# A retention + ELU kernel on one Trainium2 core: the first four chunks taken pair by pair, v scaled on GpSimd for two of them, and the fifth first-layer tile in two parts

## The chip, the core and the metric

The kernel runs on one core of a Trainium2 chip. A core has a matrix engine (TensorE, "PE" in the profile, with its weight loads as "PEld"), three engines that work on whole tiles (VectorE "DVE", ScalarE "ACT", GpSimd "POOL") and SyncE ("SP"), which here issues every DMA transfer. Each engine runs its own queue in order and waits for the others through semaphores. The metric is device time in microseconds of one execution, as a median over several.

## The reference

Two blocks follow each other. The first is a retention layer on q, k, v of shape (4 batches, 8 heads, 768 positions, 64 channels):

```python
for t in range(S):
    state = gamma * state + outer(k[t], v[t])      # per batch and head, gamma = 1 - 2**(-5-h)
    y[t] = q[t] @ state / sqrt(D)
```

Its output, read as x of shape (3072 tokens, 512), goes through a two-layer network with an ELU between:

```python
h = x @ w_in            # 512 -> 2048
g = where(h > 0, h, exp(min(h, 0)) - 1)
out = g @ w_out         # 2048 -> 512
```

q, k and v are float32. w_in and w_out are float64 and reach the chip as bit patterns.

## The kernel before

Tokens are worked in six blocks (`tb`) of 512 tokens, each of four chunks of 128 positions. A chunk has its q and k turned (`qk`) and its k and v as they are (`kvn`), each 0.5 MB and loaded by one DMA. Chunks of a block are taken in two pairs (`pp` = 0 and 1; `x` is the chunk in the pair), and a chunk is two halves (`sub`) of 64 positions.

**Retention of a pair.** `scale_v` multiplies v by the powers of 1/gamma (v'). `scores` (L260) forms k q^T for both halves and VectorE masks it (L273) into the place of k in `qk`. `states` (L279) forms k^T v' per half on TensorE (L290) and adds it to the state of the half before (L301, or a ScalarE copy, L299, where no state goes before); the new state is written over the k that has just been used, so state n+1 of a chunk lies in the first or second half of that chunk's k. `outputs` (L303) has three steps, run by `next(y)`: the masked scores times v' (L314) and the first half of the products of q with the states (L338, `other` = 0); then a small VectorE read of both accumulators (L326, `seen`) and the second half of the products (`other` = 1); then the multiplication by powers of gamma into `xb`, the network's input (L345).

**PSUM.** Pool `ps_r` has four buffers, given out in turn: for the first pair two to the scores, two to the states, and then two to the outputs, which are the buffers of the scores again.

**Weights.** There are 16 pieces of 1 MB: eight of w_in, then eight of w_out. `prepare` (ScalarE, L142 and L144) and `decode` (four VectorE operations, L163 to L166) turn a piece from float64 bits into float32; a piece may be taken in two parts of 512 columns. Three pieces may be staged at once, so the load of a further piece (L121) waits on SyncE for the decode that frees a buffer, and all later loads wait behind it.

**The first block.** `plain_first` (L402) forms the 16 tiles of h for block 0. Its first four tiles are done in two halves of 256 tokens, so that half 0 (the first pair) can go before the second pair's outputs are there: tiles 0 and 1 (bank `pa`, weights `w_a`[0]), tile 2 (`pb`) and tile 3 (`pd`, both of `w_b`[0]), L409. The other twelve are done with all 512 tokens at once (L420). Their ELU is two ScalarE operations (L390, L391) and one on VectorE (L394).

Each engine's order is the order in which the program issues. The order at the start is written out by hand (the lines after `second_twice`, ending in the loop over `inner`): prepare piece 0, decode its first part, scale chunks 0 and 1, scores of the first pair, decode the second part, states, prepare piece 1, outputs, scale chunk 2, decode piece 1, scale chunk 3, prepare piece 2, tiles 0 and 1 of half 0, scores and states of the second pair, first part of piece 2's decode, tiles 2 and 3 of half 0, outputs of the second pair, second part of the decode, and then the rest of the tiles with a piece decoded at every second one. v' is made on VectorE for chunks 0 and 2, by eight ScalarE operations each for chunks 1 and 3, and on GpSimd for all later ones (L242).

After block 0 the blocks use a seven-product scheme (`strassen`, `second`, `first_twice`, `second_twice`), with the retention of the next block spread between; the change leaves those lines as they are.

Of the kernel before, what the change touches and what calls it, by code (L numbers as in the profile page):

```python
# [9 lines left out]
FP32 = mybir.dt.float32  # L10
# [3 lines left out]
ALU = mybir.AluOpType  # L14
# [3 lines left out]
def kernel(  # L18
# [32 lines left out]
    nc = tc.nc  # L51
    PSUM = bass.MemoryType.PSUM
    P = nc.NUM_PARTITIONS

    B, H, S, D, DM, DFF = dims
# [3 lines left out]
    TH = TB // 2  # L59
    HP = H // 2  # L60
# [3 lines left out]
    CPB = TB // C  # L64
# [84 lines left out]

    quarters = lambda f: scratch.rearrange("(s k) p (f c) -> k f p s c", k=2, f=4)[f // 4, f % 4]  # L150

    def decode():

        n = len(decoded)
        if n >= NPIECE:
            return
        dst, todo = prepared[n]
        decoded.append(dst.rearrange("p (a b) -> p a b", a=2))
        vec = nc.vector
        for c, hi, flat in todo:  # L160
            cf = c.bitcast(FP32)

            vec.tensor_scalar(cf, cf, 122879.9921875, 2.0**-15, ALU.min, ALU.max)  # L163
            vec.tensor_scalar(c, c, 3, 0x3FFFFFF8, ALU.logical_shift_left, ALU.bitwise_and)
            vec.scalar_tensor_tensor(c, hi, 0xC0000000, c, ALU.bitwise_and, ALU.bitwise_or)
            vec.tensor_tensor(out=flat, in0=c, in1=flat, op=ALU.add)  # L166
# [81 lines left out]
    def state(tb, n):  # L248

        if n % (2 * CPB) == 0:  # L250
            return carry[(tb + n // (2 * CPB)) % 2]

        k = raw[tb * CPB + (n - 1) // 2][1][:, 0].rearrange("p h d -> p (h d)")
        return k[:, (n - 1) % 2 * 256 : ((n - 1) % 2 + 1) * 256].rearrange("p (h e) -> p h e", e=D)

    def fresh(tb, n):

        return (tb * 2 * CPB + n) % (S // D) == 0

    def scores(tb, pp):  # L260

        two = [raw[tb * CPB + 2 * pp + x][0] for x in range(2)]
        sc = [ps_r.tile([P, 2, HP, D], FP32, name="sc", tag="r") for _ in range(2)]
        for x, qk in enumerate(two):
            for p in range(HP):
                for sub in range(2):
                    for a in range(2):
                        nc.tensor.matmul(
                            sc[a][rows(sub), x, p, :], lhsT=qk[rows(a), 1, p, rows(sub)],
                            rhs=qk[rows(a), 0, p, rows(sub)], start=True, stop=True, skip_group_check=True,  # L270
                        )
        for a in range(2):
            nc.vector.tensor_tensor(  # L273
                out=two[a][:, 1].rearrange("p h c -> p (h c)").rearrange("p (n t) -> p n t", t=D),
                in0=sc[a].rearrange("p x h t -> p (x h) t"),
                in1=cmask.unsqueeze(1).to_broadcast([P, 2 * HP, D]), op=ALU.mult,
            )

    def states(tb, pp):  # L279

        kvs = [ps_r.tile([P, 2, HP, D], FP32, name="kv", tag="r") for _ in range(2)]
        order = [(x, sub) for x in range(2) for sub in range(2)]
        last = lambda x, sub: fresh(tb, 4 * pp + 2 * x + sub + 1)
        for x in range(2):
            kv = raw[tb * CPB + 2 * pp + x][1]
            for p in range(HP):
                for sub in range(2):
                    for a in range(2):
                        if not last(x, sub):
                            nc.tensor.matmul(  # L290
                                kvs[sub][rows(a), x, p, :], lhsT=kv[rows(sub), 0, 2 * p + a, :],
                                rhs=kv[rows(sub), 1, 2 * p + a, :], start=True, stop=True, skip_group_check=True,
                            )
        for x, sub in order:
            n = 4 * pp + 2 * x + sub
            if last(x, sub):
                continue
            if fresh(tb, n):
                nc.scalar.copy(state(tb, n + 1), kvs[sub][:, x])  # L299
            else:  # L300
                nc.vector.tensor_tensor(out=state(tb, n + 1), in0=kvs[sub][:, x], in1=state(tb, n), op=ALU.add)  # L301

    def outputs(tb, pp):  # L303

        y = [ps_r.tile([P, 2 * 2, 2, D], FP32, name="y", tag="r") for _ in range(2)]
        for x in range(2):
            kv = raw[tb * CPB + 2 * pp + x][1]
            for j in range(4):
                a, u = divmod(j, 2)
                pt = raw[tb * CPB + 2 * pp + a][0][:, 1].rearrange("p h c -> p (h c)")  # L310
                for sub in range(2):
                    for c in range(2):
                        p = 2 * u + c
                        nc.tensor.matmul(  # L314
                            y[sub][rows(c), j, x, :], lhsT=kv[rows(sub), 1, head(a, u, c), :],
                            rhs=pt[rows(sub), (x * HP + p) * D : (x * HP + p + 1) * D],
                            start=(x == 0 and j == 0), stop=False, skip_group_check=True,
                        )
        for other in range(2):
            if not other:  # L320
                yield
            else:

                for sub in range(2):
                    seen = epool.tile([P, 8], FP32, name="seen", tag="seen")
                    nc.vector.tensor_copy(seen.rearrange("p (j x) -> p j x", x=2), y[sub][:, :, :, 0])  # L326
                yield
            for x in range(2):
                q = raw[tb * CPB + 2 * pp + x][0]
                for u in range(2):  # L330
                    for a in range(2):
                        sub = a ^ other
                        n = 4 * pp + 2 * x + sub
                        if fresh(tb, n):
                            continue
                        for c in range(2):
                            p = 2 * u + c
                            nc.tensor.matmul(  # L338
                                y[sub][rows(c), 2 * a + u, x, :], lhsT=state(tb, n)[rows(a), p, :],
                                rhs=q[rows(a), 0, p, rows(sub)], start=False, stop=True, skip_group_check=True,  # L340
                            )
        i = chunks[tb * CPB + 2 * pp][1]
        for sub in range(2):
            place = lambda t: t.rearrange("p j (x s c) -> p j x s c", x=2, s=2)[:, :, :, sub, :]
            nc.vector.tensor_tensor(  # L345
                out=place(xb[:, :, 2 * pp * C : 2 * (pp + 1) * C]), in0=y[sub],
                in1=place(etab.rearrange("p a u t -> p (a u) t")[:, :, i * C : (i + 2) * C]), op=ALU.mult,
            )
# [53 lines left out]
    def plain_first():  # L402
# [1 line left out]
        tiles = [(n, w, row, fi) for n in range(NQ) for w, row in ((w_a, 0), (w_b, 1)) for fi in range(2)]  # L404
        banks = [bank(x) for x in "aabd"]
        for t in range(2):
            for (n, w, row, fi), hp in zip(tiles, banks):
                for j in range(4):
                    nc.tensor.matmul(  # L409
                        hp[:, t, :], lhsT=w[n][:, fi, j // 2, j % 2, :], rhs=xb[:, j, half[t]],  # L410
                        start=(j == 0), stop=(j == 3), skip_group_check=True,
                    )
                if t == 1:
                    elu(g_plain[row * NF + 2 * n + fi], hp.rearrange("p a b -> p (a b)"))
                if t == 1 or fi == 1:
                    yield
        for n, w, row, fi in tiles[4:]:
            hp = ps_r.tile([P, TB], FP32, name="hp", tag="r")
            for j in range(4):
                nc.tensor.matmul(  # L420
# [525 lines left out]
    next(y)  # L946
    next(y)
    next(y, None)
    next(piece)
    next(piece, None)  # L950
    prepare()
# [230 lines left out]
```

## Time and profile before

| what | value |
|---|---|
| median of 5 executions | 651.57 us (650.21 to 653.41) |
| the profiled execution | 653.41 us, the longest of the five; span 651.6 us |
| mean granted TensorE clock | 0.995 |
| TensorE busy | 633.2 us (97%) |
| VectorE, ScalarE, GpSimd busy | 469.5, 237.7, 37.0 us |
| moved by DMA | 134.16 MB, mean 206 GB/s |

The profiled execution lasted 1.8 us longer than its span; that is time outside the first and the last instruction. In the timeline views a row gives the start in us from the span's start, the time from the first start to the last end of a run of like instructions, engine, line, operation, the tiles, shapes, the count, and in brackets the idle time before it and what ended it. One matrix product of the program shows as two MATMUL and two LDWEIGHTS rows. "issue" is idle time for which the profile shows nothing that was waited for. In the table of windows, PEclk is the share of the TensorE clock that was granted.

### The profile page before, as it was taken

To read this page: it belongs to the slowest core of one execution; us is meant where nothing else is said; L and a number is where in the kernel's file an instruction comes from. 1 tells how busy PE (TensorE), PEld (TensorE's weight loads), DVE (VectorE), ACT (ScalarE), POOL (GpSimd) and SP (SyncE) were. 2 spreads that over 40 slices of the span, in tenths; PEclk is the share of its full clock that TensorE was granted. 3 is DMA by queue.
4 is the path that set the end of the run, shared out by engine and by line. 5 is a ranking of instruction groups with operands and counts; after the bars stand their busy time and mean duration, and the time that the engine had idled before them with its cause. 6 is when DMAs were issued, how large, how long until landed. Compare 5 with 4: busy or idle time off the path is not lost.

```text
span 651.6 us, 15255 instructions
## 1 busy us (share of the span) xinstructions
PE 633.2 (97%) x6336; PEld 538.9 (83%) x6336; DVE 469.5 (72%) x829; ACT 237.7 (36%) x447; POOL 37.0 (6%) x36
## 2 busy tenths in 40 slices
PE   4889999999999999999999999999999999999998
PEld 3664445548888889989989988999988999988997
DVE  5688778757866845489857578958569958557976
ACT  7466733104542001455111455311355311256311
POOL 1000100000540000020000020000020000000000
PEclk9799999999999999999999999999999999999999
DMA  8638979537293784931778830688850588610694
GB/s 341 242 130 287 308 238 278 146 103 258 65 323 137 245 298 156 375 134 34 246 244 280 289 155 4 205 267 283 281 210 3 174 268 266 226 56 1 209 307 164
DMA packets 69012, 134.16 MB, mean 206 GB/s; under 512 B 5712, under 2 KB 23504, under 8 KB 66640
## 3 DMA queue, kind: packets, MB, share of 16 engines
q1 hardware_dynamic: 68944, 133.19, 60.6%
q8 instruction: 50, 0.82, 0.5%
q14 instruction: 18, 0.15, 0.1%
HBM read 109.05 MB, written 24.12 MB: 204 GB/s over the span
## 4 chain that ended last, share of the span: by engine, by line
PE 96%; DMA 1%; DVE 1%; issue 1%; SPq 0%; DVEq 0%
PE pa L780 16%; PE pa L741 10%; PE pd L780 8%; PE hp L420 6%; PE pa L695 4%; PE pa L434 4%; PE pa L579 4%; PE pb L741 4%; PE pa L521 4%; PE pb L780 4%; PE qa L741 3%; PE pd L695 2%; PE pd L579 2%; PE qd L741 2%; PE pd L521 2%; PE pd L741 2%
## 5 line engine op out<-in xcount | busy, mean ns | idle before, releaser
L788 ACT COPY ms<-pa 128x128 f32<-128x128 f32 x83 | 22.1, 266 | 114.8 <-PE pa L780 114.8
L391 ACT ACTIVATE r<-r 128x512 f32<-128x512 f32 x96 | 60.5, 630 | 3.1
L780 PE MATMUL pa<-ts,wq 128*128 128x128 f32 x448 | 59.2, 275 | 0.0
L780 PE MATMUL pd<-ts,wq 128*128 128x128 f32 x440 | 58.2, 275 | 0.0
L780 PEld LDWEIGHTS pa<-ts,wq 128*128 128x128 f32 x448 | 54.8, 192 | 0.2
L780 PEld LDWEIGHTS pd<-ts,wq 128*128 128x128 f32 x440 | 53.5, 192 | 0.2 <-DVE res L792 0.2
L780 PE MATMUL pa<-gC,wq 128*128 128x128 f32 x384 | 51.9, 278 | 1.6 <-issue 1.6
L390 ACT ACTIVATE r<-gC 128x512 f32<-128x512 f32 x64 | 39.9, 624 | 33.8 <-DVE gC L749 33.8
L780 PEld LDWEIGHTS pa<-gC,wq 128*128 128x128 f32 x384 | 47.3, 192 | 2.7 <-issue 1.7
L394 DVE SCALAR_TENSOR_TENSOR gC<-r,gC 128x512 f32<-128x512 f32 x64 | 45.8, 748 | 0.7 <-ACT r L391 0.7
L242 POOL TENSOR_TENSOR kvn<-kvn,vf 128x512 f32<-128x512 f32 x20 | 23.0, 1154 | 361.8 <-DMA kvn<-in_qkv_dram 197.8
L471 ACT COPY m<-pa 128x512 f32<-128x512 f32 x27 | 15.7, 581 | 60.8 <-PE pa L579 35.5
L792 DVE TENSOR_TENSOR res<-pd,ms 128x128 f32<-128x128 f32 x54 | 15.4, 286 | 29.0 <-PE pd L780 28.4
L657 DVE TENSOR_TENSOR ts<-gC,ts 128x512 f32<-128x512 f32 x48 | 33.0, 687 | 0.8
L657 DVE TENSOR_TENSOR ts<-gC 128x512 f32<-128x512 f32 x48 | 32.7, 682 | 0.0
L434 PE MATMUL pa<-gC,w_s 128*128 128x512 f32 x64 | 30.6, 600 | 0.0
L579 PE MATMUL pa<-gC,ws 128*128 128x256 f32 x128 | 28.6, 381 | 0.0
L579 PEld LDWEIGHTS pa<-gC,ws 128*128 128x128 f32 x128 | 24.1, 190 | 3.4
L780 PE MATMUL pb<-gC,wq 128*128 128x128 f32 x192 | 26.4, 277 | 0.1
L780 PEld LDWEIGHTS pb<-gC,wq 128*128 128x128 f32 x192 | 23.7, 192 | 0.8 <-DVE gC L394 0.8
L749 DVE TENSOR_TENSOR gC<-qa,gC 128x512 f32<-128x512 f32 x8 | 5.5, 692 | 25.1 <-PE qa L741 18.3
L813 ACT COPY res<-pa 128x128 f32<-128x128 f32 x27 | 7.2, 266 | 44.7 <-PE pa L780 42.3
(199 smaller groups left out, 1293.2 us busy)
## 6 DMA issues: line engine op xcount, KB each, us to landing
wq<-scratch_dram SPq DMA_DIRECT2D x228, 256.0 KB, 4.3
wraw<-in_w_dram SPq DMA_DIRECT2D x16, 1024.0 KB, 5.8
qk<-in_qkv_dram SPq DMA_DIRECT2D x24, 512.0 KB, 7.2
kvn<-in_qkv_dram SPq DMA_DIRECT2D x24, 512.0 KB, 7.9
scratch_dram<-so SPq DMA_DIRECT2D x22, 512.0 KB, 3.2
ws<-scratch_dram SPq DMA_DIRECT2D x7, 1024.0 KB, 7.9
scratch_dram<-w_s SPq DMA_DIRECT2D x8, 512.0 KB, 7.1
out_dram<-res SPq DMA_DIRECT2D x11, 256.0 KB, 4.3
```

The source lines that it names most:

```text
L242: eng.tensor_tensor(out=kv[:, 1], in0=kv[:, 1], in1=vf[:, i].unsqueeze(2).to_broadcast([C, H, D]), op=ALU.mult)
L390: nc.scalar.activation(e, h, AF.Relu, scale=-1.0)
L391: nc.scalar.activation(e, e, AF.Exp, scale=-1.0)
L394: nc.vector.scalar_tensor_tensor(g, e, -1.0, h, ALU.add, ALU.max)
L420: nc.tensor.matmul(hp, lhsT=w[n][:, fi, j // 2, j % 2, :], rhs=xb[:, j, :], start=(j == 0), stop=(j == 3))
L434: nc.tensor.matmul(ops[d], lhsT=wo[:, row, d * P : (d + 1) * P], rhs=g_plain[row * NF + f], start=(f == 0 and row == 0), stop=(f == NF - 1 ...
L521: nc.tensor.matmul(ps[:, fi, :], lhsT=w[:, fi, j2, :], rhs=x[:, j2, :], start=(begin and fi == 0 and j2 == 0), stop=(j2 == 1), skip_group_ ...
L579: nc.tensor.matmul(ps[:, d, :], lhsT=ws[:, 2 * d + f // 4, f % 4, :], rhs=gq[INPUT2[j]][:, f, :], start=(begin and f == 0 and d == 0), sto ...
L657: sub = lambda o, x, y: nc.vector.tensor_tensor(out=o, in0=x, in1=y, op=ALU.subtract)
L695: nc.tensor.matmul(ps[:, f, :], lhsT=lhs[f], rhs=xs[j][k], start=(begin and f == 0), stop=True, skip_group_check=True,)
L741: nc.tensor.matmul(ps[:, fi, :], lhsT=w[:, fi, j2, :], rhs=x[:, j2, :], start=(j in (1, 7) and fi == 0 and j2 == 0), stop=(j2 == 1), skip_ ...
L780: nc.tensor.matmul(ps, lhsT=w[:, f, :], rhs=ts[j][k][:, f, :], start=(begin and f == 0), stop=(f == 3), skip_group_check=True,)
```

## The change

- **First pair by chunks.** Scores, masks, states and outputs of block 0's first pair are issued chunk by chunk: scores of chunk 0, its mask, its k^T v', then scores of chunk 1, the states after chunk 0, the mask of chunk 1. The mask becomes four operations of 128x256 in place of two of 128x512, and a chunk's masked scores lie in its own `qk`. The outputs become five steps: L314's products of chunk 0, those of chunk 1, then the two halves of the state products, then the multiplication into `xb`.
- **k^T v' of chunk 1** is split by half: that of its first half goes between the two chunks' L314 products, that of its second half behind the outputs' last product, and its addition behind the multiplication into `xb`. The state between the two halves (state 3) goes to `xt[0]`, which is free then, since k is still needed.
- **v'** of chunks 1 and 2 is made on GpSimd (before: eight ScalarE operations, and one on VectorE). Chunk 0 stays on VectorE and chunk 3 on ScalarE.
- **Decode of piece 0** can be stopped after each VectorE operation: the second part's first two operations go behind the mask of chunk 1, the third behind the addition of state 3, the fourth behind the `seen` copies.
- **Tile 4** of `plain_first` (`w_a`[1], first 512 columns of piece 2) is done in two halves of 256 tokens too. Its half 0 is issued after the second pair's outputs.

```diff
-    def decode():
+    def decode(fine=False):
...
             vec.tensor_scalar(cf, cf, 122879.9921875, 2.0**-15, ALU.min, ALU.max)
+            if fine:
+                yield
...
-        if m in (1, 3):
+        if m == 3:
...
-        eng = nc.vector if m < CPB else nc.gpsimd
+        eng = nc.vector if m == 0 else nc.gpsimd
...
+        if (tb, n) == (0, 3):
+
+            return xt[0].rearrange("p a t -> p (a t)")[:, 0:256].rearrange("p (h e) -> p h e", e=D)
...
+    def mask_pair(sc, x):
+
+        place = raw[x][0][:, 1].rearrange("p h c -> p (h c)").rearrange("p (a n t) -> p a n t", a=2, t=D)
+        for a in range(2):
+            nc.vector.tensor_tensor(
+                out=place[:, a], in0=sc[a][:, x], in1=cmask.unsqueeze(1).to_broadcast([P, HP, D]), op=ALU.mult
+            )
...
         for t in range(2):
-            for (n, w, row, fi), hp in zip(tiles, banks):
+            for k, (n, w, row, fi) in enumerate(tiles[:5]):
+                if k == 4 and t == 0:
+                    banks.append(ps_r.tile([P, 2, TH], FP32, name="hp", tag="r"))
+                hp = banks[k]
...
-                if t == 1 or fi == 1:
+                if t == 1 or k in (1, 3, 4):
                     yield
-        for n, w, row, fi in tiles[4:]:
+        for n, w, row, fi in tiles[5:]:
...
+    def take(count=1):
+        for _ in range(count):
+            next(piece, None)
+
     prepare(2)
-    piece = decode()
-    next(piece)
+    piece = decode(True)
+    take(4)
+    sc = [ps_r.tile([P, 2, HP, D], FP32, name="sc", tag="r") for _ in range(2)]
+    score_products(sc, 0, 0, 0)
     scale_v(0)
     scale_v(1)
-    scores(0, 0)
-    next(piece)
-    next(piece, None)
-    states(0, 0)
+    mask_pair(sc, 0)
+    kvs = [ps_r.tile([P, 2, HP, D], FP32, name="kv", tag="r") for _ in range(2)]
+    state_products(kvs, 0, 0, 0, range(2))
+    score_products(sc, 0, 0, 1)
+    state_sum(kvs, 0, 0, 0, 0)
+    state_sum(kvs, 0, 0, 0, 1)
+    mask_pair(sc, 1)
+    take(2)
     prepare()
-    y = outputs(0, 0)
+    y = outputs(0, 0, True)
+    next(y)
+    state_products(kvs, 0, 0, 1, [0])
+    next(y)
+    state_sum(kvs, 0, 0, 1, 0)
+    take()
+
     next(y)
     next(y)
+    state_products(kvs, 0, 0, 1, [1])
+    take(2)
     next(y, None)
+    state_sum(kvs, 0, 0, 1, 1)
     scale_v(2)
     decode_all()
     scale_v(3)
...
     next(y)
     next(y)
     next(y, None)
+    next(inner)
     next(piece)
     next(piece, None)
     prepare()
```

`score_products`, `state_products` and `state_sum` are the loops of `scores` and `states` taken out as functions, for one chunk, for chosen halves, and for one addition.

More of the change, by code (lines that the diff above doesn't have):

```diff
@@ L163, in decode @@
             vec.tensor_scalar(cf, cf, 122879.9921875, 2.0**-15, ALU.min, ALU.max)
+            if fine:
+                yield
             vec.tensor_scalar(c, c, 3, 0x3FFFFFF8, ALU.logical_shift_left, ALU.bitwise_and)
+            if fine:
+                yield
             vec.scalar_tensor_tensor(c, hi, 0xC0000000, c, ALU.bitwise_and, ALU.bitwise_or)
+            if fine:
+                yield
             vec.tensor_tensor(out=flat, in0=c, in1=flat, op=ALU.add)
@@ L258, in fresh, with score_products @@
         return (tb * 2 * CPB + n) % (S // D) == 0
+    def score_products(sc, tb, pp, x):
+        qk = raw[tb * CPB + 2 * pp + x][0]
+        for p in range(HP):
+            for sub in range(2):
+                for a in range(2):
+                    nc.tensor.matmul(
+                        sc[a][rows(sub), x, p, :], lhsT=qk[rows(a), 1, p, rows(sub)],
+                        rhs=qk[rows(a), 0, p, rows(sub)], start=True, stop=True, skip_group_check=True,
+                    )
     def scores(tb, pp):
-        two = [raw[tb * CPB + 2 * pp + x][0] for x in range(2)]
         sc = [ps_r.tile([P, 2, HP, D], FP32, name="sc", tag="r") for _ in range(2)]
[L264 to L271, printed above, removed]
+        for x in range(2):
+            score_products(sc, tb, pp, x)
         for a in range(2):
             nc.vector.tensor_tensor(
-                out=two[a][:, 1].rearrange("p h c -> p (h c)").rearrange("p (n t) -> p n t", t=D),
+                out=raw[tb * CPB + 2 * pp + a][0][:, 1].rearrange("p h c -> p (h c)").rearrange("p (n t) -> p n t", t=D),
                 in0=sc[a].rearrange("p x h t -> p (x h) t"),
@@ L277, in scores, with state_products @@
             )
+    def mask_pair(sc, x):
+        place = raw[x][0][:, 1].rearrange("p h c -> p (h c)").rearrange("p (a n t) -> p a n t", a=2, t=D)
+        for a in range(2):
+            nc.vector.tensor_tensor(
+                out=place[:, a], in0=sc[a][:, x], in1=cmask.unsqueeze(1).to_broadcast([P, HP, D]), op=ALU.mult
+            )
+    def state_products(kvs, tb, pp, x, subs):
+        kv = raw[tb * CPB + 2 * pp + x][1]
+        for p in range(HP):
+            for sub in subs:
+                for a in range(2):
+                    if not fresh(tb, 4 * pp + 2 * x + sub + 1):
+                        nc.tensor.matmul(
+                            kvs[sub][rows(a), x, p, :], lhsT=kv[rows(sub), 0, 2 * p + a, :],
+                            rhs=kv[rows(sub), 1, 2 * p + a, :], start=True, stop=True, skip_group_check=True,
+                        )
@@ L279, in states, with state_sum @@
+    def state_sum(kvs, tb, pp, x, sub):
+        n = 4 * pp + 2 * x + sub
+        if fresh(tb, n + 1):
+            return
+        if fresh(tb, n):
+            nc.scalar.copy(state(tb, n + 1), kvs[sub][:, x])
+        else:
+            nc.vector.tensor_tensor(out=state(tb, n + 1), in0=kvs[sub][:, x], in1=state(tb, n), op=ALU.add)
     def states(tb, pp):
         kvs = [ps_r.tile([P, 2, HP, D], FP32, name="kv", tag="r") for _ in range(2)]
-        order = [(x, sub) for x in range(2) for sub in range(2)]
@@ L283, in states @@
-        last = lambda x, sub: fresh(tb, 4 * pp + 2 * x + sub + 1)
         for x in range(2):
[L285 to L303, printed above, removed]
+            state_products(kvs, tb, pp, x, range(2))
+        for x in range(2):
+            for sub in range(2):
+                state_sum(kvs, tb, pp, x, sub)
@@ L305, in outputs @@
+    def outputs(tb, pp, first=False):
         y = [ps_r.tile([P, 2 * 2, 2, D], FP32, name="y", tag="r") for _ in range(2)]
@@ L309, in outputs @@
                 a, u = divmod(j, 2)
-                pt = raw[tb * CPB + 2 * pp + a][0][:, 1].rearrange("p h c -> p (h c)")
+                pt = raw[tb * CPB + 2 * pp + (x if first else a)][0][:, 1].rearrange("p h c -> p (h c)")
                 for sub in range(2):
@@ L315, in outputs @@
                             y[sub][rows(c), j, x, :], lhsT=kv[rows(sub), 1, head(a, u, c), :],
-                            rhs=pt[rows(sub), (x * HP + p) * D : (x * HP + p + 1) * D],
+                            rhs=pt[rows(sub), ((a if first else x) * HP + p) * D :][:, 0:D],
                             start=(x == 0 and j == 0), stop=False, skip_group_check=True,
                         )
+            if first and x == 0:
+                yield
         for other in range(2):
@@ L341, in outputs @@
                             )
+        if first:
+            yield
         i = chunks[tb * CPB + 2 * pp][1]
```

## The prediction

> **What bounds the kernel now.** I read the page's busy line first, then the waits of TensorE in the first 45 us, its timeline there, the table of windows for the clock, and the timelines of VectorE and ScalarE, from which the times without a fence come.
>
> ```profile
> PE 633.2 (97%) x6336; PEld 538.9 (83%) x6336; DVE 469.5 (72%) x829; ACT 237.7 (36%) x447; POOL 37.0 (6%) x36
> q8 instruction: 50, 0.82, 0.5%
> ```
>
> TensorE is idle for only 651.6 - 633.2 = 18.4 us. Its waits from 7 to 45 us hold most of it (9.0 us there are the first loads of qk, which the change doesn't touch):
>
> ```profile
> PE sc L268 <- DMA qk<-in_qkv_dram: 9.0, 2, 7.5
> PE pa L409 <- DVE xb L345: 2.8, 2, 1.4
> PE y L338 <- issue: 1.3, 1, 1.3
> PE y L338 <- DVE seen L326: 0.6, 2, 0.3
> ```
>
> From 35.70 us TensorE is without a gap for hundreds of us, so what it gains before 36 us reaches the end unless something later becomes late. Its timeline:
>
> ```profile
> 10.09 1.13 PE L268 MATMUL sc<-qk 64*64 64x64 f32 x32 [1.42 <-DMA qk<-in_qkv_dram]
> 11.00 2.88 PE L290 MATMUL kv<-kvn 64*64 64x64 f32 x61
> 16.38 0.44 PE L338 MATMUL y<-qk,kvn 64*64 64x64 f32 x6 [0.27 <-DVE seen L326]
> 18.12 0.80 PE L338 MATMUL y<-qk,kvn 64*64 64x64 f32 x18 [1.30 <-issue]
> 20.34 5.68 PE L409 MATMUL pa<-xb,w_a 128*128 128x256 f32 x16 [1.41 <-DVE xb L345]
> 25.94 1.16 PE L268 MATMUL sc<-qk 64*64 64x64 f32 x64
> 33.57 0.69 PE L338 MATMUL y<-qk,kvn 64*64 64x64 f32 x32 [0.33 <-DVE seen L326]
> 35.70 3.72 PE L409 MATMUL pa<-xb,w_a 128*128 128x256 f32 x16 [1.44 <-DVE xb L345]
> 39.26 1.89 PE L409 MATMUL pb<-xb,w_b 128*128 128x256 f32 x8
> 40.99 1.89 PE L409 MATMUL pd<-xb,w_b 128*128 128x256 f32 x8
> 42.72 7.03 PE L420 MATMUL hp<-xb,w_a 128*128 128x512 f32 x16
> ```
>
> Two things are to be seen besides the waits on `xb`. In the middle of L338 the engine stands for 1.30 us with nothing to wait for. The DMA view of 15.5 to 16.8 us has one packet of the instruction queue, of 0.02 MB, beside data that fill the 16 engines to 99.0%. 0.82 MB in 50 packets carry some 12,700 matmul and weight-load rows, about 253 each. I read the stall as TensorE having run out of instructions, with the refill held up by the loads. And the same 16 products `pa` take 5.68 us at 20.34 and 3.72 at 35.70; the windows say why:
>
> ```profile
> 14.11:17.52 3.41, 2.31 (x88) 1.81 (x83) 2.12 (x6) 2.48 (x3) 0.00 (x0) 1.00 1.03 408
> 17.52:20.94 3.42, 1.40 (x20) 1.12 (x20) 1.95 (x4) 0.60 (x3) 0.00 (x0) 0.50 1.04 428
> 20.94:24.35 3.41, 3.41 (x10) 2.69 (x9) 3.31 (x4) 2.92 (x9) 0.00 (x0) 0.50 0.64 262
> ```
>
> The granted clock (third column from the end) is half from 17.5 to 24.35 us, after a window with TensorE idle for a third of it.
>
> **Part 1, the first pair.** In order, with durations from the rows; 32 small products start within 0.91 us (10.09 to 11.00) early and 64 within 0.99 us (25.94 to 26.93) later.
> - v' of chunk 0 is unchanged and ends at 10.12 (0.69 us from 9.44). k^T v' of chunk 0 starts then, 0.91 us, so the scores of chunk 1 go from 11.1 to 12.0, and are there at 12.25, 1 us later than before (11.22).
> - ScalarE's copy (0.37) and one VectorE addition (0.42) end at 12.2. The two masks of chunk 1, priced by L301's same shape at 0.42, end at 13.1; before, two masks of 0.69 ended at 12.58. Four smaller masks for two cost 0.3 us on VectorE.
> - L314's products need the scores' PSUM buffers back, so both masks of chunk 1 release them: 13.1 against 13.54. 32 products, 16 of k^T v', 32 more: 0.9 + 0.45 + 0.5 to 0.9, ends at 14.9 to 15.3. v' of chunk 1 comes from GpSimd: kv of chunk 1 was there at 11.4, L242 there takes 1.04 to 1.49 us, so 12.5 to 12.9, not late for its use at 14.0. ScalarE loses 2.02 us of work (to 13.45) that ended last for the products before.
> - VectorE: decode 0.43 + 0.43 to 14.0, addition of state 3 to 15.1, decode 0.69 to 15.8, `seen` 0.25 to 16.05. Before it was 16.34. **So the second half of the state products may start some 0.3 us earlier.** The decode that moved (2.3 us stood ahead of the additions) is mostly made up for by the chunks' chain.
> - The stall. Before L338's stop at 18.12, 192 + 30 = 222 small products had started. In the new order 200 precede the second half of L338's products, so the 222nd is the 22nd of its 24. [...] The loads up to 14.8 us are the same. So I take the refill at the same 18.1 us. Then 2 products remain where 18 did (0.80 us): `xb` starts at 18.12 + 0.05 + 0.35 = 18.5, not 18.99; the first `pa` at 19.85, not 20.34. The cost of k^T v' of the second half (16 products, 0.45 us) lies in TensorE's wait for `xb`.
> - `pa` at half clock: at full clock 16 take 35.70 to 39.26 = 3.56 us; each us at half clock loses 0.5. From 19.85 to 24.35 that is 2.25, so 5.81 against 5.60 before, and the next scores start at 25.66: **0.28 us gained**.
>
> What moved past others: the load behind piece 0 (L121) waits on SyncE for the last decode, 16.6 in place of 14.83. Behind it is only the load after piece 1. The DMA engines are full until 22.8 us anyway; its data are used by a decode at 39.6. GpSimd's v' of chunk 2 waits for its data, with nothing behind it until 62 us. Bounds: nothing to 1.2 us late, used at 26.9, so hidden. Decode of piece 1 (3.84 us) starts after `xb` and one addition, at 20.3, ends at 24.1, used at 27.7: hidden.
>
> [...]
>
> **Part 2, tile 4.** L338 starts its last 32 at 33.57, 0.5 us, so TensorE is free from 34.07 to 35.70: 1.63 us. Half a tile is 8 products, 1.73 us (39.26 to 40.99). The weights are decoded at 32.5 and its buffer was freed at 29.9. It fills the wait and ends 0.1 us beyond `xb`. Later the tile costs 1.73 where it cost 3.43 (half of 42.72 to 49.58). **Gain 0.18 at 35.7 (with part 1's), then 1.70: 1.88 us in sum.** Bounds of this part: -0.1 (nothing filled) to 1.63.
>
> **Later.** VectorE is nearly always busy from 35.6 to 59.7, so it will not follow TensorE. Its decode of `w_b`[1] ends at 43.61 and is used at 49.58, 6 us; with TensorE 1.7 us ahead 4 remain, and later pieces have 8 and more. The ELU of tile 4 ended 49.9, its buffer is used at 56.45. Nothing becomes late.
>
> **Sum.** 653.41 - 1.9 = 651.5 for the profiled execution, the longest of five; on the median, 651.57 - 1.9 = 649.7 us.
>
> **The rivals.**
> - *The stall goes.* If the refill is there earlier (it is DMA timing), `xb` starts at 16.7 and `pa` at 18.0; half clock from 17.52 to one full window later, 20.94, loses 1.5: ends 23.1 against 25.94, 2.9 us, with part 2 4.5: 647.1 us. v' of chunk 3 (22.4) and piece 2 (loaded at 22.8) would not be late. For it: other refills are not seen to stop TensorE for over 0.2 us up to 300 us. Against: the same instruction count and the same loads. [...]
> - *The clock.* The window from 17.52 to 20.94 or the one before may now count as busy: `pa` loses 0.5 to 2.2 us less. 649.7 less these: 647.5 to 649.2. The windows' place differs between executions.
> - *Part 2 gives nothing.* The half tile waits for its weights (32.5, were VectorE over 1.6 us later) or a later unit takes it back: 0.3 us gained, 651.3.
> [...]
>
> **How the numbers follow.** Likeliest case 0.55, stall gone 0.1, clock 0.15, nothing from part 2 0.1, slower 0.1. 0.3% is 1.95 us, about what a measurement of this kernel can tell from no change; it lies at 649.6, so the likeliest case falls near half on either side (0.26 and 0.29). Faster: 0.26 + 0.1 + 0.14 = 0.5; same: 0.29 + 0.01 + 0.1 + 0.01 = 0.41; slower 0.09. The range runs from the stall's rival, 647.0, to 652.3, the median with part 2 lost and half of VectorE's 1.42 us on the path.
>
> **What would show it.** Right: one issue stall in L338 that ends near 18.1, with few products behind it; `xb` L345 at about 18.5; `pa` L409 at 19.9; a `hp` row of 8 products of 128x256 right behind L338 at about 33.8 and no wait for `xb` near 35; GpSimd's L242 ending by 12.9. Wrong: a stall elsewhere or none; a wait of L314 or L290 on GpSimd; VectorE's first decode operations at twice their time; `hp` waiting for the decode; new idle time of TensorE after 40 us.

## The result, and the profile after

| | before | changed |
|---|---|---|
| median | 651.65 us (649.51 to 654.09) | 649.56 us (646.90 to 652.54) |
| profiled execution: span | 651.6 us | 647.9 us |
| ratio of the times, 95% interval | | 0.9970 (0.9961 to 0.9978) |

The changed kernel is 2.1 us faster; the forecast was 649.7 us, 1.9 us faster. The two profiled executions lie 3.7 us apart, more than the medians: single executions of one kernel spread over 5 us, and the experiments show two things that differ between them, the first rise of the clock and the stops of TensorE.

TensorE's waits from 7 to 45 us of the changed kernel (us in all, times, longest):

```profile
PE sc L274 <- DMA qk<-in_qkv_dram: 7.5, 1, 7.5
PE kv L305 <- DVE kvn L248: 1.4, 1, 1.4
PE pa L441 <- DVE xb L374: 0.7, 1, 0.7
PE y L365 <- DVE seen L353: 0.6, 2, 0.3
PE y L339 <- DVE qk L295: 0.5, 1, 0.5
```

The stop named "issue" is not there, and one of the two waits for `xb` is gone. The timeline of TensorE:

```profile
12.58 1.34 PE L339 MATMUL y<-qk,kvn 64*64 64x64 f32 x30 [0.53 <-DVE qk L295]
16.51 0.76 PE L365 MATMUL y<-qk,kvn 64*64 64x64 f32 x12 [0.27 <-DVE seen L353]
19.05 5.92 PE L441 MATMUL pa<-xb,w_a 128*128 128x256 f32 x16 [0.72 <-DVE xb L374]
24.90 1.16 PE L274 MATMUL sc<-qk 64*64 64x64 f32 x64
32.53 0.69 PE L365 MATMUL y<-qk,kvn 64*64 64x64 f32 x32 [0.33 <-DVE seen L353]
33.16 1.99 PE L441 MATMUL hp<-xb,w_a 128*128 128x256 f32 x8
34.99 3.62 PE L441 MATMUL pa<-xb,w_a 128*128 128x256 f32 x16
47.06 7.03 PE L452 MATMUL hp<-xb,w_b 128*128 128x512 f32 x16
```

The first `pa` starts at 19.05 (20.34 before), the next scores at 24.90 (25.94), and the half of tile 4, `hp` at 33.16, is followed by the other tiles without a gap. Tile 6 starts at 47.06 (49.58). The second half of the state products starts no earlier than before (16.51, before 16.38): up to there the first pair has gained nothing. Its gain is the 1.30 us for which TensorE stood behind that point before. The windows of the clock (third column from the end):

```profile
13.32:16.73 3.41, 3.14 (x100) 2.95 (x94) 1.97 (x6) 2.31 (x2) 0.00 (x0) 1.00 1.02 405
20.15:23.56 3.41, 3.41 (x10) 2.69 (x9) 2.96 (x3) 2.63 (x9) 0.00 (x0) 1.00 0.84 346
```

These print 1.00, but here the column misleads: this trace holds no clock record before 23.56 us, where the first one, of full clock, begins. The rows above show the half clock: `pa` takes 5.92 us, where 3.62 is its time at full clock. So in this execution the clock rose only at 23.56. GpSimd, ScalarE and VectorE:

```profile
11.46 1.04 POOL L248 TENSOR_TENSOR kvn<-kvn,vf 128x512 f32<-128x512 f32 x1 [8.75 <-DMA kvn<-in_qkv_dram]
17.86 1.04 POOL L248 TENSOR_TENSOR kvn<-kvn,vf 128x512 f32<-128x512 f32 x1 [5.37 <-DMA kvn<-in_qkv_dram]
```

```profile
11.23 0.37 ACT L315 COPY kvn<-kv 128x256 f32<-128x256 f32 x1 [2.90 <-PE kv L305]
```

```profile
12.10 0.76 DVE L295 TENSOR_TENSOR qk<-sc,cmask 128x256 f32<-128x256 f32 x2
14.73 0.42 DVE L317 TENSOR_TENSOR xt<-kv,kvn 128x256 f32<-128x256 f32 x1 [1.07 <-PE kv L305]
17.71 1.29 DVE L374 TENSOR_TENSOR xb<-y,etab 128x512 f32<-128x512 f32 x2 [0.66 <-PE y L365]
33.32 1.29 DVE L374 TENSOR_TENSOR xb<-y,etab 128x512 f32<-128x512 f32 x2 [0.84 <-PE y L365]
```

v' of chunk 1 is ready at 12.50 us. No VectorE operation beside these two is longer than elsewhere in this profile: the addition at 11.63 takes 0.42 us, the two masks at 12.10 take 0.76 (0.75 at 9.92), the two `xb` at 17.71 take 1.29, as at 33.32. No decode operation stood beside either. In the kernel before, one beside L242 (62.20 us, for 1.37) took 1.41 us, and 0.69 to 0.70 in its 13 other rows of that shape; from it come the 1.42 us (2 x 0.71) of the forecast's range:

```profile
62.70 1.41 DVE L164 TENSOR_SCALAR wraw<-wraw 128x1024 uint32<-128x1024 uint32 x1
```

### The profile page after: what moved, and what is told of

Its sections match the earlier page's. It is cut to its first block, busy times and chain, and to the rows that moved or that the text cites. A ratio compares the mean times of both kernels' runs of the same rounds, so it can differ in the third digit from the quotient of the medians.

```text
span 647.9 us, 15272 instructions
## 1 busy us (share of the span) xinstructions
PE 633.7 (98%) x6344; PEld 541.0 (84%) x6344; DVE 470.5 (73%) x830; ACT 235.6 (36%) x439; POOL 39.2 (6%) x38
## 4 chain that ended last, share of the span: by engine, by line
PE 97%; DVE 1%; ACT 1%; DMA 1%; issue 0%; POOL 0%; SPq 0%; POOLq 0%
PE pa L812 16%; PE pa L773 10%; PE pd L812 8%; PE hp L452 6%; PE pa L466 4%; PE pa L611 4%; PE pb L773 4%; PE pa L553 4%; PE pa L727 4%; PE pb L812 4%; PE qa L773 3%; PE y L339 2%; PE pd L611 2%; PE qd L773 2%; PE pd L773 2%; PE pd L553 2%
## 5 line engine op out<-in xcount | busy, mean ns | idle before, releaser
L248 POOL TENSOR_TENSOR kvn<-kvn,vf 128x512 f32<-128x512 f32 x22 | 25.2, 1149 | 356.1 <-DMA kvn<-in_qkv_dram 346.3
L781 DVE TENSOR_TENSOR gC<-qa,gC 128x512 f32<-128x512 f32 x8 | 5.5, 692 | 24.5 <-PE qa L773 18.3
```

Source lines behind the costliest of these rows:

```text
L248: eng.tensor_tensor(out=kv[:, 1], in0=kv[:, 1], in1=vf[:, i].unsqueeze(2).to_broadcast([C, H, D]), op=ALU.mult)
```

## The experiments

Ratios are to the kernel before, run on the same chip in turn with the experiment, with 95% intervals. Its median differed between the three groups of experiments (651.45, 651.88 and 652.86 us), so ratios are compared and not times.

**Part 1 alone.** Tile 4 in one piece again:

```diff
-            for k, (n, w, row, fi) in enumerate(tiles[:5]):
+            for (n, w, row, fi), hp in zip(tiles, banks):
...
-    next(inner)
     next(piece)
```

> Part 1 alone: the first pair by chunks, v' on GpSimd and the stopped decode, but tile 4 in one piece as before. My theory: the two parts add up; part 1 brings xb L374 forward by 0.5 us if a refill stall stands in the second half of the state products, and by about 1.3 us (as in the profile of the changed kernel) if none does. Expected: 0.3 to 1.0 us less than before, ratio 0.9985 to 0.9995; the wait of TensorE for xb near 34 us is back at 1.4 us. Rival (part 1 is nearly all of the gain): 2 us less, ratio 0.997.

Ratio 0.9989 (0.9974 to 1.0003). In its timeline the first `pa` starts at 18.68 us and the wait for the second `xb` is back:

```profile
32.50 5.41 PE L438 MATMUL pa<-xb,w_a 128*128 128x256 f32 x16 [1.44 <-DVE xb L374]
```

This `pa` takes 5.41 us: the trace has a window at half clock from 33.46 to 36.87. The ratio is in the range expected for part 1, less than half of the gain, but its interval reaches from no change to nearly all of the gain (0.9970), so it doesn't tell the two theories apart.

**Tile 4 alone.** The kernel before with the loop over `tiles[:5]` and the added `next(inner)`.

> Part 2 alone: the kernel before with tile 4 in two halves, half 0 behind the second pair's outputs. My theory: it fills the 1.63 us in which TensorE stands at 34 us; 1.6 us less than before, ratio 0.9975, and the first products pa stay near 20.3 us. Rival (VectorE takes it back later, or part 2 needs the earlier decode of part 1): 0 to 0.5 us less, ratio over 0.999.

Ratio 1.0011 (0.9990 to 1.0032): the expected gain is not in the time. Yet the profile has it. No wait for `xb` is left near 34 us (second `xb` started at 33.99), and tile 6 follows 13.74 us after it:

```profile
33.83 1.99 PE L412 MATMUL hp<-xb,w_a 128*128 128x256 f32 x8
35.66 3.62 PE L412 MATMUL pa<-xb,w_a 128*128 128x256 f32 x16
47.73 4.46 PE L423 MATMUL hp<-xb,w_b 128*128 128x512 f32 x10
```

Before, it was 49.58 - 34.36 = 15.22 us; in the changed kernel it is 47.06 - 33.32 = 13.74. So the fill is worth 1.5 us on the spot. Of its lead, 0.8 us is lost near 331 us, where this profile has a stop of TensorE of 2.32 us, and before's one of 1.55 (before's row first):

```profile
334.86 0.60 PE L780 MATMUL pa<-gC,wq 128*128 128x128 f32 x3 [1.55 <-issue]
333.01 0.33 PE L338 MATMUL y<-qk,kvn 64*64 64x64 f32 x3 [2.32 <-issue]
```

The profiled execution still ends 1.0 us before the one of the kernel before (650.6 against 651.6 us). Why the median of twelve executions has none of it stays open.

**The two halves without the fill.** The halves of tile 4 stand one behind the other, after the second halves of the first four:

```diff
-        for t in range(2):
-            for (n, w, row, fi), hp in zip(tiles, banks):
+        for t, k in [(t, k) for t in range(2) for k in range(4)] + [(0, 4), (1, 4)]:
```

> The kernel before with tile 4 in two halves that stand one behind the other, so that nothing fills the wait for xb at 34 us; TensorE has 8 MATMUL and 8 LDWEIGHTS rows more. My theory of tile 4 alone: the fill gains 1.5 us up to 285 us, and the 16 rows more move the end of an instruction page near 330 us 16 rows ahead in the program, into the small products there, which costs up to 0.75 us. Then this kernel is 0 to 0.8 us slower than before and its stop near 330 us stands in L338. Rival (two halves are dearer by themselves, and that is why tile 4 alone shows no gain): 1.5 us or more slower, with the loss in the first 60 us.

Ratio 1.0025 (1.0006 to 1.0045). From second `xb` to tile 6 it takes 15.24 us, before 15.22, so two halves are not dear in themselves, and up to 285 us it is no later than before (scores of block 3 at 284.85, before 285.68). The loss in this profile is at 331 us, with the clock at half behind it from 334.5 to 337.9:

```profile
334.28 0.34 PE L338 MATMUL y<-qk,kvn 64*64 64x64 f32 x3 [2.57 <-issue]
334.55 1.86 PE L782 MATMUL pa<-gC,wq 128*128 128x128 f32 x7
```

The stop stands in L338, as expected; the price was larger than my 0.75 us (1.0 us of longer stop, and half clock behind it), and the ratio, 1.6 us by before's median (0.4 to 2.9 by its interval), is above the 0 to 0.8 us that I expected.

**Tile 4 alone, once more.**

> Tile 4's split alone once more, for a second profile. My theory: against the same kernel with the halves together, its last first-layer tiles start 1.4 to 1.7 us earlier after L338 at 34 us, and it gives that back near 330 us, where the end of an instruction page now stands in the small products of L338 (product 3133), with a stop of 1.5 to 2.6 us where the kernel before has 1.56 us; median within 0.4 us of before either way or above it. Rival (chance in the first 12 executions): no stop near 330 us is longer than before's, and the median falls to 1.3 us or more below before.

Ratio 0.9993 (0.9974 to 1.0012). Tile 6 again follows the second `xb` by 13.74 us, but this profile has no stop near 331 us and a span of 648.7 us. So the stop is not there each time: my expectation of a regular one falls, and so does the rival's median. What is left: alone, the split gives no gain that these times show.

**v' as before.** Chunk 1 on ScalarE, chunk 2 on VectorE again:

```diff
-        if m == 3:
+        if m in (1, 3):
...
-        eng = nc.vector if m == 0 else nc.gpsimd
+        eng = nc.vector if m < CPB else nc.gpsimd
```

> The changed kernel with v' of chunk 1 on ScalarE and of chunk 2 on VectorE again. My theory: GpSimd's v' ends at 12.5 us and is used at 13.6 us, ScalarE's would end near 13.5 us, so chunk 1 is no later; VectorE's 0.68 us for chunk 2 delays a decode that has 2 us to spare. Expected: equal to the changed kernel within 0.3 us, ratio to the kernel before 0.9965 to 0.9975. Rival (the move to GpSimd carries part 1): the products of chunk 1 wait, xb comes 0.5 us or more later, ratio 0.998 or above.

Ratio 1.0003 (0.9986 to 1.0021): the gain is gone, my theory falls, and the rival is right about the size. Its mechanism was not v' itself. The timelines of ScalarE, VectorE and TensorE:

```profile
11.42 2.02 ACT L245 ACTIVATE kvn<-kvn,vf 128x64 f32<-128x64 f32 x8 [3.10 <-DMA kvn<-in_qkv_dram]
13.34 0.35 ACT L315 COPY kvn<-kv 128x256 f32<-128x256 f32 x1
```

```profile
13.73 0.42 DVE L317 TENSOR_TENSOR kvn<-kv,kvn 128x256 f32<-128x256 f32 x1 [3.07 <-ACT kvn L315]
14.07 0.75 DVE L295 TENSOR_TENSOR qk<-sc,cmask 128x256 f32<-128x256 f32 x2
```

```profile
14.54 1.34 PE L339 MATMUL y<-qk,kvn 64*64 64x64 f32 x30 [2.50 <-DVE qk L295]
```

State 1 is copied by ScalarE, and in the new order that copy stands behind the eight operations of v'. It starts at 13.34, in the changed kernel at 11.23. VectorE's addition of state 2 waits for it, the masks of chunk 1 stand behind that addition, and the outputs wait 2.50 us for the masks' buffers in place of 0.53. The second half of the state products starts at 18.46 us (changed 16.51, before 16.38): without the move the new order is some 2 us behind the old one, with it level.

**Decode held together.**

```diff
     mask_pair(sc, 1)
-    take(2)
+    take(5)
```

with the later `take` lines left out.

> The changed kernel with all four operations of the second part of piece 0's decode behind the mask of chunk 1, none held back. My theory: they end at 15.0 us, the addition of state 3 starts at 15.0 in place of 14.73, and the seen copies follow the state products at once: xb moves by 0.3 us or less, and the time by 0.3 us or less either way. Rival (the holding back carries the gain of part 1): the seen copies and xb come 0.7 us or more later, ratio to before 0.9985 or above.

Ratio 0.9966 (0.9948 to 0.9983), no different from the changed kernel. State 3 is added at 15.15 (14.73), the `seen` copies start at 16.23 (16.11):

```profile
15.15 0.42 DVE L317 TENSOR_TENSOR xt<-kv,kvn 128x256 f32<-128x256 f32 x1
16.23 0.35 DVE L353 COPY seen<-y 128x8 f32<-128x8 f32 x2 [0.66 <-PE y L365]
```

Holding the decode back is worth 0.1 us here.

**All of k^T v' ahead.**

```diff
-    state_products(kvs, 0, 0, 1, [0])
+    state_products(kvs, 0, 0, 1, range(2))
...
-    state_products(kvs, 0, 0, 1, [1])
```

> The changed kernel with k^T v' of both halves of chunk 1 ahead of its second L339 products, none behind the outputs; 16 MATMUL and 16 LDWEIGHTS rows move ahead of the state products. My theory: 0.45 us of small products at half clock come onto the path to the seen copies, and the 222nd product now falls 16 products earlier in the second half of the state products, where TensorE arrives at or just after 17.0 us; xb starts 0.3 to 0.6 us later (18.0 to 18.3), time 0.2 to 0.6 us more than the changed kernel. Rival (those products lie beside VectorE's work and cost nothing): xb at 17.4 to 17.8 us and no difference.

Ratio 0.9968 (0.9952 to 0.9985), and `xb` at 17.61 us: the rival's numbers came. Its reason is not shown: the second half of the state products does start 0.3 us later (16.83 to 16.51), and in this profile the clock rose at 16.30 and the rest is shorter (rows of 0.22 to 0.26 us from 17.11 on, where the changed kernel's first profile has 0.32).

**Small products ahead of all.** The kernel before with 50 products of 64x64 before the first scores:

```diff
+    idle = bank("b")[0:D, 0, 0:D]
+    for _ in range(50):
+        nc.tensor.matmul(
+            idle, lhsT=causal[0:D, 0:D], rhs=causal[0:D, 0:D], start=True, stop=True, skip_group_check=True
+        )
```

> The kernel before with 50 products of 64x64 (100 MATMUL and 100 LDWEIGHTS rows) ahead of the first scores, in the time in which TensorE waits for its first load; their result is not used. My theory: the stop of 1.30 us in L338 is a refill of instructions that comes late while the loads fill the DMA engines; 200 more instructions put the first refill ahead of the loads, so it ends before 7 us, no stop stands in the first pair's L338, and xb L345 starts at 17.0 to 17.5 us in place of 19.0; 1 to 1.9 us less than before, ratio 0.997 to 0.9985; a part of it may come from the clock, which may rise earlier. Rival (the stop belongs to this place in the program, not to the count of instructions): a stop of about 1.3 us in L338 stays, ratio 1.000. Second rival (the refill is late whatever its place): a stop stands some 100 products earlier or later and the time does not fall.

Ratio 1.0047 (1.0028 to 1.0065). I mis-sized it: 99 rows took 10.82 us, so the first scores came at 13.28 and all that follows late. The first refill packet started at 14.09 us (before: 15.61), not before 7 us as I expected. No stop is seen in the first pair, but TensorE was late itself, so it settles nothing on that stop.

**Idle products ahead of the first pair.** The changed kernel with ten products of 128x128 ahead of the scores, three behind them, four behind the last k^T v':

```diff
+    def idle_products(count):
+        idle = bank("b")[:, 0, 0:P]
+        for _ in range(count):
+            nc.tensor.matmul(idle, lhsT=causal, rhs=causal, start=True, stop=True, skip_group_check=True)
...
+    idle_products(10)
     prepare(2)
...
     score_products(sc, 0, 0, 0)
+    idle_products(3)
...
     state_products(kvs, 0, 0, 1, [1])
+    idle_products(4)
```

> The changed kernel with ten products of 128x128 ahead of the first scores, three behind them and four behind the last k^T v' of chunk 1; their results are not used. The clock's theory: the ten keep TensorE busy from 2.8 to 7.2 us, so the full clock is granted before the first pair and the small products and pa run fast; by that alone 2 us less than the changed kernel. The theory of the refill: 52 rows more stand ahead, so TensorE reaches the end of its first instructions near the first outputs' state products, while the refill is usable only near 17 to 18 us as before; a stop of 1.5 to 3 us stands there, some 26 small products earlier in the program, and xb starts at 18.3 us or later, no earlier than without. Together: pa faster, xb later: 0 to 1.5 us less than the changed kernel. Rival (the stop is tied to the place in the program or is chance): no stop ahead of the seen copies, and the time falls by 2 us or more.

Ratio 0.9983 (0.9967 to 0.9998). The clock rose at 8.04 us and fell to half again from 18.28 to 21.69, so `pa` took 4.41 us. The stop came where the theory put it:

```profile
14.03 0.23 PE L365 MATMUL y<-qk,kvn 64*64 64x64 f32 x2
16.61 0.33 PE L365 MATMUL y<-qk,xt 64*64 64x64 f32 x4 [2.35 <-issue]
```

222 MATMUL rows precede it, idle ones counted, as they did in the kernel before. `xb` starts at 17.97, no earlier than without; my 18.3 was a little high.

**Idle products behind only.** Five, then two, behind the last k^T v':

```diff
     state_products(kvs, 0, 0, 1, [1])
+    idle_products(5)
```

> The changed kernel with five products of 128x128 behind the last k^T v' of chunk 1, in the time in which TensorE waits for the first xb; their result is not used. My theory (the clock follows how busy a fixed window of 3.41 us was): the window in which pa starts counts as busy, the full clock is granted one window earlier than in the changed kernel's profile (23.56 us), the 16 products pa take 4.2 to 5.0 us in place of 5.85, and the time falls by 0.5 to 1.7 us against the changed kernel: 648 to 649. Rival (the clock looks back over longer, or the products delay pa): no change or up to 0.5 us slower.

Ratio 0.9955 (0.9939 to 0.9971). They delay the first `pa` to 20.60, with `xb` there at 19.04, but it takes 4.21 us; the next scores come at 24.74, in the changed kernel's first profile at 24.90.

> The changed kernel with two idle products of 128x128 behind the last k^T v' of chunk 1, where five delayed the first pa to 20.62 us (xb was there at 19.06). My theory: two last about 1 us at half clock, so pa starts at 19.1 to 19.4 us, the window before it still counts as busy, and the clock is full by about 20 us; 0 to 1.2 us less than with five: 647.6 to 648.9, and less than the changed kernel by 0.7 us or more. Rival (two are too few to count, the window was carried by five): the clock rises only in the window after, pa takes near 5.9 us, time as the changed kernel, 649.5 to 650.4.

Ratio 0.9933 (0.9912 to 0.9953), 648.04 us. Its interval lies below the changed kernel's 0.9961 to 0.9978, so by the ratios **it beats both kernels**; it has six executions, and the changed kernel was not run beside it (its two variants in the same group gave 0.9966 and 0.9968).

```profile
18.29 1.22 PE L959 MATMUL pb<-causal 128*128 128x128 f32 x4
19.30 4.74 PE L441 MATMUL pa<-xb,w_a 128*128 128x256 f32 x16
23.97 1.16 PE L274 MATMUL sc<-qk 64*64 64x64 f32 x64
```

`pa` is not held up, TensorE is busy through the window from 18.17, and the clock rises at 21.58. The expected "by about 20 us" missed: it rises at the window's end. The next scores come 0.93 us earlier than in the changed kernel's first profile, but 1.63 us later than in its second (22.34, below), so one profile doesn't show that the clock makes the gain of the median.

**The changed kernel again.**

> The changed kernel as it is, for a second profile. My theory: TensorE's stop in the second half of the state products comes where it reaches its 222nd small product before the instruction refill is there (refill's end plus 1.3 to 1.4 us); it passes that product near 17.2 us, so a refill that ends after 15.9 us stops it there, one that ends before does not. xb starts at 17.4 to 18.6 us. Near 330 us the same rule holds at product 3133. Rival: the stops have no fixed product; then one would stand elsewhere. Time 649.0 to 650.2 us.

Ratio 0.9976 (0.9958 to 0.9994), 650.39 us, just above the expected range; the first `xb` starts at 17.35, just below it. The front is faster than in the first profile, because the clock rose at 16.27 and stayed:

```profile
18.69 3.72 PE L441 MATMUL pa<-xb,w_a 128*128 128x256 f32 x16 [0.92 <-DVE xb L374]
22.34 1.16 PE L274 MATMUL sc<-qk 64*64 64x64 f32 x64
```

Tile 6 starts at 45.18 us. But at 328.6 us TensorE stops for 1.77 us at product 3133, and the span is the same 647.9 us. The rival has a point too: at 29.40 us TensorE stops for 0.43 us after 476 rows, which is neither of the two counts.

**The stops together.** From the traces: the end of the packet of the instruction queue nearest before, and the stop of TensorE, both in us, with the MATMUL rows ahead of it.

| kernel | rows ahead | packet ends | stop | from packet's end |
|---|---|---|---|---|
| before | 222 | 16.72 | 16.82 to 18.12 | 1.40 |
| tile 4 alone | 222 | 16.87 | 17.35 to 18.32 | 1.45 |
| halves without fill | 222 | 16.24 | 17.00 to 17.53 | 1.30 |
| tile 4 alone, again | 222 | 16.07 | 16.83 to 17.28 | 1.21 |
| idle ahead | 222 | 15.23 | 14.26 to 16.61 | 1.39 |
| before | 3133 | 333.62 | 333.31 to 334.86 | 1.25 |
| tile 4 alone | 3133 | 331.64 | 330.69 to 333.01 | 1.37 |
| halves without fill | 3133 | 332.90 | 331.71 to 334.28 | 1.38 |
| changed, again | 3133 | 329.02 | 328.56 to 330.33 | 1.32 |
| decode together | 3133 | 331.35 | 331.14 to 332.64 | 1.29 |
| v' as before | 3133 | 331.98 | 332.87 to 333.32 | 1.34 |

Part 1 alone has a stop of 1.12 us after 3132 rows. Four more stand at other counts: 0.43 and 0.16 us after 476 rows (changed, again; part 1 alone), 0.72 us after 4389 (50 small products ahead) and 0.79 us after 5267 (idle ahead). In the table the stops stand at the same counts of rows, whatever the program does there, and end 1.21 to 1.45 us after a packet of the instruction queue. Where no stop is seen at product 222 or 3133, in any of the 14 profiles, it starts 1.3 us or more after the packet's end (222 in the changed kernel's first profile: 17.27, the packet's end 15.64). I read the two together as refills that come late; no row names a cause. In the first pair, packets end at 16.1 to 16.9 us in kernels with the order before, and at 15.6 to 16.0 us in those with the new one (idle products ahead: 15.23; 50 small products ahead of the order before: 15.14). Why, and what sets the start of the one near 330 us (322 to 332.6 us), I could not tell apart.

## Why the prediction was right, and where it wasn't

- **The sum** (1.9 us off the median) measured 2.1 us. Its terms came out differently, and part of the agreement is luck. The upper end of the range was not what its words say: 651.57 + 0.71 = 652.3 leaves out part 1's 0.28 us too; with it the end is 652.0.
- **Part 2** ("1.63 us of wait, filled") holds as a mechanism. From second `xb` to tile 6 it gave 1.5 us (not 1.70) in all ten profiles that have it: 13.73 to 13.74 us, against 15.22 to 15.24 in three without it (the fourth has 16.90, with a window at half clock). In the medians it isn't settled: alone 1.0011 and 0.9993; on top of part 1, from 0.9989 to 0.9970, with intervals that overlap. "Nothing becomes late" failed: I followed data and not instructions, and the stop at 3133 rows stood in the profile before, as a wait of 1.55 us that the prediction left out. A load became late too: the changed kernel's first profile has a wait of 0.42 us for `wq` at 257.4 us, where before's has none. In the three profiles of tile 4's split with part 1's front as before, that stop was 2.32, 2.57 and 0 us.
- **The stall in part 1** is the step that failed: "I take the refill at the same 18.1 us". The reading of the stop fits the runs: the count of 222 holds in every stop of the first pair. But the packet ends at 15.64 us in the new order (before 16.72), so by the 1.2 to 1.5 us of the table the refill is usable near 17.0 us; TensorE starts the product at 17.27 us, and nothing stops. When a refill is asked for, no run shows; the traces show its packet, which started at 14.53 us here and at 15.61 before. In the profiles of the new order it ended at 15.2 to 16.0 us, so nothing spoke for the 0.1 of "slower". `xb` started at 17.71, not 18.5. The rival "the stall goes" had this at 0.1. The first `pa` gained 1.29 us; its slower run took 0.25 of that (5.85 us to the next scores, before 5.60), so the gain at the next scores was 1.0 us, not 0.28 and not 2.9.
- **The order itself** gained nothing up to there. "The second half of the state products may start some 0.3 us earlier" failed: it started at 16.51 us, 0.13 later than before. It started at 16.38 to 16.91 us in four profiles with the order before and at 16.48 to 16.83 in seven with the new one and v' on GpSimd. The first `xb` of the order before, less the length of its stop, would stand at 17.4 to 17.9 us in those four (18.99 - 1.30, 17.85 - 0.44); the new order has 17.33 to 17.83. So what part 1 gains at the first `xb` is the stop. Two things keep it away: the packet ends earlier (15.6 to 16.0 us in place of 16.1 to 16.9), and the product comes later in the second half. Why the packet is earlier stays open.
- **The clock.** 5.81 us for the first `pa` against 5.85 measured, by luck and for a wrong reason: a rise at 24.35 was assumed, and the trace has 23.56 with none before. The second profile has 3.65 us. The rival "the clock" (0.5 to 2.2 us less) occurs in some executions; it was no separate case but a spread.
- **GpSimd.** Ready at 12.5 us as priced. Of the 1.42 us of VectorE in the range nothing came: beside the two v' its operations kept their length, and no decode stood there. The sum had nothing for it. But I gave the move no worth. Without it the new order loses 2.0 us at the first `pa` (21.01 against 19.05) and its whole gain in time (1.0003), since the move clears ScalarE's queue for the copy of state 1. I had counted what stood ahead of VectorE's additions, and not what stands ahead of ScalarE's copy.
- **The decode and the late k^T v'** were priced at 0.3 and 0.45 us on or beside the path; each is worth nothing that the times show.

## What to carry to other kernels

When work is moved from one engine to another, list what stood behind it on the engine that it leaves: here, in the new order, a copy of 0.37 us that waited for 2.02 us of scaling cost 2.0 us. Before a gain is put down to a new order, compare marks ahead of and behind each stop: here the order was level with the old one, and the gain was a stop that did not come. A gain of 2 us is to be followed to the end of the program: single profiles spread by more than that, so each term is read between two marks on the same engine (here from second `xb` to tile 6, the same to 0.02 us in every profile at full clock). Two idle products in TensorE's wait ahead of a long row gave the lowest ratio of all (0.9933, six executions), while thirteen further ahead and four behind gave 0.9983; that the clock makes the difference is not shown.

## What the runs showed of the hardware that I had not expected

- TensorE stopped, with nothing in the profile that it waited for, after the same numbers of MATMUL rows in several profiles (222 in five, 476 in two, 3133 in six), for 0.2 to 2.6 us each time, in or right behind rows of some 90 small products or more. At 222 and 3133 it went on 1.21 to 1.45 us after the end of a 0.02 MB packet of the instruction queue. That it had run out of instructions is my reading.
- With 52 and 200 rows more ahead the first refill packet started at 14.12 and 14.09 us, at 14.5 to 15.8 us in the other profiles, so at most 1.7 us earlier, while the loads filled the DMA engines (mean busy share 1.02 to 1.07 from 14 to 16 us).
- In these profiles the granted clock changed only at marks 3.41 us apart or a multiple of it (before: 14.11, 17.52, 24.35), whose place differed between executions (first recorded rise at 13.62 to 27.23 us, 8.04 with idle products ahead). TensorE idle for 2.57 us at 331.7 us was followed by 3.41 us of half clock; idle for 2.32 us at 330.7 us in tile 4 alone, it kept the full clock. Each rise came behind a window in which TensorE was busy for 3.24 to 3.42 us; but with 50 small products ahead it was busy throughout from 3.93 us, and the first rise is at 17.58. Nor does the busy time tell a fall: 2.31 us of a window were followed by half clock before, 2.23 us by full clock in the changed kernel's second profile.
- Products of 64x64 took 0.11 us a row where all wrote one place (99 in 10.82 us), and 0.03 us where they alternated between four (32 in 0.91 us), both ahead of the first recorded rise of the clock; that the place is the cause was not tried.
